# Windowed attention and a squared-ReLU MLP on one core: how K, Q and V reach TensorE (casting six-row loads for two batches, fp32 loads with engine casts and bf16 transposes for the other six)

## The chip, the cores and the metric

The kernel runs on one core of a Trainium2 chip. The metric is device time in microseconds (us) of one execution; lower is better. The core has five engines that run their own instruction streams in order: TensorE (PE, with its weight loads shown as PEld), VectorE (DVE), ScalarE (ACT), GpSimd (POOL) and SyncE (SP), which here issues DMAs. POOL issues DMAs too, and only POOL's queue converts types on the way.

## The reference, cut to what matters

```python
# q, k, v: (8, 8, 576, 64) float32; global_idx: 8 sorted positions
scores = scale * np.matmul(q, k.transpose(0, 1, 3, 2))
mask = np.abs(pos[:, None] - pos[None, :]) <= 32
mask = mask | is_global[:, None] | is_global[None, :]
scores = np.where(mask, scores, -1000000000.0)
attn = softmax(scores)                              # over the keys
attn_out = np.matmul(attn, v)
x = attn_out.transpose(0, 2, 1, 3).reshape(4608, 512)
h = x @ w_in                                        # (512, 2048)
r = np.maximum(h, 0.0)
out = (s * (r * r) + b) @ w_out                     # (2048, 512), float32
```

Each query sees the keys within 32 positions and the 8 global keys; the 8 global queries see every key. The attention output of all heads is the input of the MLP.

## The kernel before, in words

**Padding.** The 576 positions of a batch are cut in five chunks (`NCH`) of 120 keys (`KC`). A chunk takes 128 rows: rows 0 to 7 hold the 8 global keys, rows 8 to 127 the chunk's own. For queries the 8 global rows sit in the middle, at rows 60 to 67. So a band of scores, chunk by chunk, holds the window and the globals together, and a multiplicative mask of zeros and ones (`masks`, one for each chunk) takes care of the rest.

**Pairs.** The work of attention is cut in 32 pairs `p`, two heads of one batch each (`bi, hp = divmod(p, 4)`). `run_pair` has eight steps `s`: steps 0 to 4 are the five chunks (`qk`: one matmul into `pss`, an exponential on ACT into `e`, the mask product on DVE into `em`); step 5 transposes K of the next pair (`trans_a`), step 6 transposes Q of the next pair (`trans_b`), step 7 multiplies by V (`pv`, into `po`). Normalisation (`norm_steps`: `ln`, `rep` on ACT, `xt` on DVE) of a pair is spread over steps 1, 3 and 4 of the next one. In batch 0, `select_globals` fetches the 8 global K and Q rows by one-hot matmuls in fp32 (`psg`), and `select_v` does it for V (`psv`).

**Row loads.** `natk` and `natq` are fp32 tiles, double buffered, filled by SP DMAs of 64-element runs (`load_k`, `load_q`); V goes by casting POOL DMAs straight into `vbufs`, a bf16 tile that holds beside each head's 64 columns 64 ones, so that `pv` gives the row sums as well. K and Q are transposed in fp32 by TensorE with an fp32 identity; ACT and DVE copy the transposes to bf16 (`kt`, `qbd`). For batches 1 to 7 the global rows come from small DRAM buffers (`gsk`, `gsq`, `gsv`), written by 24 gathers on POOL with positions held in registers, and are put into place by `fill`.

**MLP.** `moe_quanta` yields 288 quanta of four 512-column matmuls, for nine tiles of 512 tokens: per tile 16 quanta of the first product (`psh`, ReLU on ACT into `r`, square on DVE into `g`), then 16 of the second (`pso`, four of them for each 128 output rows, which DVE scales into `osb` and SP stores). `Q(n)` emits n quanta between the steps of attention, as far as the budget `quanta` allows. A tile can start when the batches that it covers have been finished by `finish_batch`, which divides the sums of the global queries and lets POOL write 8 columns of `xt`.

**Order.** The order on each engine is the order in the program, written out by hand (`manual_schedule`). DVE work of a step is collected in `later` and emitted one step later. The program is: transposes for pair 0; pairs 0 to 3 without quanta; `finish_batch(0)`; 14 quanta, with `weights_out` between them (w_out arrives in fp32 through two staging buffers, ACT casts it to `wout_t`, DVE adds it up in `wsum` for the bias row); pairs 4 to 7 with three quanta each; pairs 8 to 31 with eight quanta each; 7 quanta; `finish_batch(7)`; the last 64 quanta. Loads of the next batch are emitted ahead of its second pair (`hp == 1`).

PSUM tiles rotate: `ps_s` has two buffers, for scores and transposes; `ps_m` three, for the MLP and the selections; `po` has one.

Of the kernel before, what the change touches and what calls it, by code (L numbers as in the profile page):

```python
# [9 lines left out]
FP32 = mybir.dt.float32  # L10
# [25 lines left out]
PADROW = 96  # L36

# [22 lines left out]
def kernel(  # L60
# [24 lines left out]
    gpa = ctx.enter_context(tc.tile_pool(name="gpa", bufs=1))  # L85
    mop = ctx.enter_context(tc.tile_pool(name="mop", bufs=3))
    wtmp = ctx.enter_context(tc.tile_pool(name="wtmp", bufs=2))
# [24 lines left out]
    natk = [const.tile([P, NCH, H, D], FP32, name=f"natk{i}", tag=f"natk{i}") for i in range(2)]  # L112
    natq = [const.tile([P, NCH, H, D], FP32, name=f"natq{i}", tag=f"natq{i}") for i in range(2)]
    vbufs = [
        const.tile([P, NCH, H, 2 * D], BF16, name=f"vx{i}", tag=f"vx{i}") for i in range(2)
    ]
    qbufs = [const.tile([P, 2, LQ], BF16, name=f"qbd{i}", tag=f"qbd{i}") for i in range(3)]
    HG = H // 2
    for half in range(2):
        hs = slice(HG * half, HG * half + HG)  # L120
        nc.vector.memset(natk[0][:, :, hs], 0.0)
        nc.gpsimd.memset(natq[0][:, :, hs], 0.0)
        if half == 0:
            nc.gpsimd.memset(vbufs[0][:], 1.0)  # L124

    rowi = const.tile([P, 1], FP32)
    nc.gpsimd.iota(
        rowi[:], pattern=[[0, 1]], base=0, channel_multiplier=1,
        allow_small_or_imprecise_dtypes=True,
    )  # L130
    kidx = const.tile([P, NCH], FP32)
    nc.gpsimd.iota(
        kidx[:], pattern=[[KC, NCH]], base=0, channel_multiplier=0,
        allow_small_or_imprecise_dtypes=True,
    )
    WM = P + 2 * WIN
    iot = const.tile([P, WM], FP32)
    nc.gpsimd.iota(
        iot[:], pattern=[[1, WM]], base=-WIN, channel_multiplier=0,
        allow_small_or_imprecise_dtypes=True,  # L140
    )
    identf = const.tile([P, P], FP32)
    make_identity(nc, identf[:])


    def load_k(eng, bi, h0, nh):
        d = natk[bi % 2]
        for c in range(NCH):
            n = min(KC, S - KC * c)
            eng.dma_start(  # L150
                out=d[NG : NG + n, c, h0 : h0 + nh],
                in_=k[bi, h0 : h0 + nh, KC * c : KC * c + n].rearrange("h s d -> s h d"),
            )

    def load_q(eng, bi, h0, nh, part):
        d = natq[bi % 2]
        for c in range(NCH):
            a = KC * c + HB * part
            n = min(HB, S - a)
            r = (HB + NG) * part  # L160
            eng.dma_start(
                out=d[r : r + n, c, h0 : h0 + nh],
                in_=q[bi, h0 : h0 + nh, a : a + n].rearrange("h s d -> s h d"),
            )

    def load_v(bi):
        d = vbufs[bi % 2]
        for c in range(NCH):
            n = min(KC, S - KC * c)
            nc.gpsimd.dma_start(  # L170
                out=d[NG : NG + n, c, :, 0:D],
                in_=v[bi, :, KC * c : KC * c + n].rearrange("h s d -> s h d"),
            )

    load_k(nc.sync, 0, 0, HG)
    load_q(nc.scalar, 0, 0, HG, 0)
    load_q(nc.sync, 0, 0, HG, 1)
    load_v(0)
    load_k(nc.sync, 0, HG, HG)
    load_q(nc.sync, 0, HG, HG, 0)  # L180
    load_q(nc.sync, 0, HG, HG, 1)

# [5 lines left out]
    b_bc = const.tile([P, 1], FP32)  # L188
    nc.sync.dma_start(out=s_bc[:], in_=_bcast_dram(moe_s[:], P))
    nc.sync.dma_start(out=b_bc[:], in_=_bcast_dram(moe_b[:], P))  # L190

    w_in2 = moe_w_in.rearrange("(a p) f -> p a f", p=P)
    for j in range(4):
        nc.gpsimd.dma_start(
            out=win_t[:, :, 512 * j : 512 * j + 512],
            in_=w_in2[:, :, 512 * j : 512 * j + 512],
        )
    w_out2 = moe_w_out.rearrange("(a p) n -> p a n", p=P)
    wst = []
    for j in range(2):  # L200
        wt = wtmp.tile([P, 4, DM], FP32, tag="w", name="wo")
        nc.sync.dma_start(out=wt[:], in_=w_out2[:, 4 * j : 4 * j + 4])
        wst.append(wt)

    greg_p = [
        nc.gpsimd.value_load(g32[:1, i, 0:1], min_val=0, max_val=S - 1) for i in range(NG)  # L206
    ]


    gidx_f = const.tile([P, NG], FP32)  # L210
    nc.vector.tensor_copy(out=gidx_f[:], in_=g32[:, :, 0])
    grow = const.tile([P, 1], FP32)
    nc.vector.tensor_scalar(
        out=grow[:], in0=rowi[:], scalar1=float(NG) - 0.5, scalar2=None, op0=OP.is_le
    )
    koff = const.tile([P, 1], FP32)
    nc.vector.tensor_scalar(
        out=koff[:], in0=grow[:], scalar1=-100000.0, scalar2=-float(NG), op0=OP.mult, op1=OP.add
    )
    nc.vector.tensor_tensor(out=koff[:], in0=koff[:], in1=rowi[:], op=OP.add)  # L220

    qhi = const.tile([P, 2], FP32)
    nc.vector.tensor_scalar(
        out=qhi[:, 0:1], in0=rowi[:], scalar1=float(HB) - 0.5, scalar2=-100000.0,
        op0=OP.is_ge, op1=OP.mult,
    )
    nc.vector.tensor_scalar(
        out=qhi[:, 1:2], in0=rowi[:], scalar1=float(HB + NG) - 0.5, scalar2=100000.0 - NG,
        op0=OP.is_ge, op1=OP.mult,
    )  # L230
    nc.vector.scalar_tensor_tensor(
        out=qhi[:, 0:1], in0=qhi[:, 0:1], scalar=rowi[:], in1=qhi[:, 1:2],
        op0=OP.add, op1=OP.add,
    )
    qidx = const.tile([P, NCH], FP32)
    nc.vector.tensor_scalar(
        out=qidx[:], in0=kidx[:], scalar1=qhi[:, 0:1], scalar2=None, op0=OP.add
    )
    nc.vector.tensor_scalar(
        out=kidx[:], in0=kidx[:], scalar1=koff[:], scalar2=None, op0=OP.add  # L240
    )
    selk = const.tile([P, NCH, NG], FP32)
    selq = const.tile([P, NCH, NG], FP32)
    for sel, idx in ((selk, kidx), (selq, qidx)):
        nc.vector.tensor_tensor(
            out=sel[:], in0=view(idx[:], [1, NCH], [0, NG]),
            in1=view(gidx_f[:], [0, NCH], [1, NG]), op=OP.is_equal,
        )
    selb = const.tile([P, NCH, NG], BF16)
    nc.vector.tensor_copy(out=selb[:], in_=selk[:])  # L250
# [457 lines left out]
```

## Time and profile before

| what | value |
|---|---|
| time, median of 3 runs (lowest to highest) | 438.45 us (438.01 to 438.61) |
| the profiled execution | 437.67 us; span 436.0 us |
| PE busy | 387.0 us, 89% of the span |
| DVE busy | 265.6 us, 61% |
| ACT busy | 206.7 us, 47% |
| POOL busy | 84.5 us, 19% |
| DMA | 42.00 MB in 128367 packets, mean 96 GB/s |

The page gives busy time by engine, the span in 40 slices, the DMA queues, the chain of work that ended last, and the costliest groups of instructions as "line engine operation, output <- inputs, shapes, count | busy us, mean ns of one | idle time before, and what ended it". The mean of one is a duration; pipelined instructions start closer together than that. Other views used below are the timeline (start, us, engine, line, operation), the chain in order of time (start, us, what) and busy times in windows.

### The profile page before, as it was taken

The numbers are of one execution on the slowest core, as the hardware profiler recorded it, in microseconds if no ns is written. First come the engines' busy times: TensorE is split into PE (matmuls) and PEld (weight loads), VectorE is DVE, ScalarE is ACT, GpSimd is POOL, SyncE is SP. The second block draws the span as 40 slices with busy tenths as digits, with TensorE's granted clock in tenths as the row PEclk, the third lists the DMA queues.
The fourth block names the chain that finished last, engine by engine and source line by source line (L and its number), as shares of the span: only waits on it lengthen the run. The fifth ranks groups of instructions, "written<-read, shape, count | busy, mean of one in ns | idle before, by whom it ended". The sixth has DMA issues, their size and how long they took to land.

```text
span 436.0 us, 8254 instructions
## 1 busy us (share of the span) xinstructions
PE 387.0 (89%) x3063; PEld 241.8 (55%) x3063; DVE 265.6 (61%) x650; ACT 206.7 (47%) x405; POOL 84.5 (19%) x162
## 2 busy tenths in 40 slices
PE   1686984869799999999999999999999999999996
PEld 1563761325455655775577568656755665554442
DVE  7817443597776766676677567666766775442432
ACT  1013321855556733763476447645754673360530
POOL 9744932005005001300310050005000100100000
PEclk9999999989999999999999999999999999999999
DMA  8999194499519911991396169419941000101001
GB/s 134 154 229 257 13 147 58 170 193 97 55 48 151 150 46 67 157 143 52 88 147 111 50 122 148 75 57 138 140 86 50 26 0 30 71 2 65 31 26 72
DMA packets 128367, 42.00 MB, mean 96 GB/s; under 512 B 118655, under 2 KB 120703, under 8 KB 128327
## 3 DMA queue, kind: packets, MB, share of 16 engines
q1 hardware_dynamic: 83724, 34.00, 40.7%
q0 software_dynamic: 43328, 7.16, 24.1%
q8 instruction: 24, 0.39, 0.4%
q10 hardware_dynamic: 1275, 0.31, 0.4%
q14 instruction: 16, 0.13, 0.1%
HBM read 38.82 MB, written 9.83 MB: 112 GB/s over the span
## 4 chain that ended last, share of the span: by engine, by line
issue 49%; PE 30%; POOL 10%; ACT 5%; DVE 4%; POOLq 1%; DMA 1%; ACTq 0%; DVEq 0%
PE psh L518 10%; PE pso L533 10%; POOL vx L170 4%; POOL xt L498 3%; PE psg L391 3%; PE po L450 3%; PE pst L349 2%; ACT e L427 1%; ACT r L525 1%; PE pss L423 1%; DMA wo<-in_moe_w_out_dram 1%; POOL vx L124 1%; ACT kt L363 1%; POOLq L206 1%; DVE vx L417 1%
## 5 line engine op out<-in xcount | busy, mean ns | idle before, releaser
L518 PE MATMUL psh<-xt,win_t 128*128 128x512 bf16 (+7 forms) x1024 | 145.5, 289 | 15.8 <-POOL xt L498 12.3
L533 PE MATMUL pso<-wout_t,g 128*128 128x512 bf16 x576 | 141.1, 379 | 0.0
L525 ACT ACTIVATE r<-psh 128x512 bf16<-128x512 f32 x144 | 89.5, 627 | 80.7 <-PE psh L518 77.8
L427 ACT ACTIVATE e<-pss 128x384 bf16<-128x384 f32 (+1 forms) x160 | 75.5, 484 | 106.6 <-PE pss L423 105.4
L518 PEld LDWEIGHTS <-win_t 128*128 128x128 bf16 x1024 | 86.8, 98 | 62.6 <-issue 21.3
L528 DVE TENSOR_TENSOR g<-r 128x512 bf16<-128x512 bf16 x144 | 60.6, 424 | 53.8 <-ACT r L525 51.8
L533 PEld LDWEIGHTS <-g 128*128 128x128 bf16 x576 | 55.3, 98 | 55.9
L430 DVE TENSOR_TENSOR em<-e,mask 128x384 bf16<-128x384 bf16 (+1 forms) x160 | 54.6, 342 | 36.8 <-ACT e L427 35.5
L498 POOL COPY xt<-xg 128x4 bf16 x72 | 15.7, 218 | 271.9 <-DVE xg L496 239.1
L423 PE MATMUL pss<-qbd,kt 128*128 128x384 bf16 (+1 forms) x160 | 51.4, 337 | 12.1 <-POOL qbd L302 4.0
L542 DVE SCALAR_TENSOR_TENSOR osb<-pso,s_bc,bias_row 128x512 f32<-128x512 f32 x36 | 26.9, 747 | 31.8 <-PE pso L533 31.8
L381 DVE CAST qbd<-pst 64x512 bf16<-64x512 f32 x64 | 44.1, 689 | 2.1 <-PE pst L349 1.2
L450 PE MATMUL po<-em,vx 128*64 128x160 bf16 (+3 forms) x896 | 37.1, 233 | 3.1 <-DVE vx L417 1.7
L450 PEld LDWEIGHTS <-vx 128*64 128x64 bf16 x896 | 29.7, 117 | 14.5 <-issue 7.9
L349 PE MATMUL pst<-identf,natk 128*128 128x128 f32 x160 | 30.0, 295 | 8.7 <-DMA natk<-in_k_dram 8.6
L170 POOL DMA_DIRECT2D vx<-in_v_dram x40 | 35.3, 897 | 3.2 <-issue 3.2
L349 PE MATMUL pst<-identf,natq 128*128 128x128 f32 x160 | 28.8, 298 | 5.7 <-ACT kt L363 4.8
L349 PEld LDWEIGHTS pst<-identf,natk 128*128 128x128 f32 x160 | 20.9, 150 | 18.7 <-POOL identf masks.py:199 8.6
L481 DVE TENSOR_TENSOR xt<-po,rep 128x600 bf16<-128x600 f32 x32 | 25.1, 783 | 8.6 <-ACT rep L479 8.6
L423 PEld LDWEIGHTS <-kt 128*128 128x128 bf16 x160 | 15.5, 100 | 25.8 <-DVE qbd L381 6.1
L363 ACT CAST kt<-pst 128x512 bf16<-128x512 f32 x32 | 20.1, 629 | 18.2 <-PE pst L349 18.2
L349 PEld LDWEIGHTS pst<-identf,natq 128*128 128x128 f32 x160 | 19.7, 150 | 11.6 <-ACT kt L363 9.1
(75 smaller groups left out, 202.0 us busy)
## 6 DMA issues: line engine op xcount, KB each, us to landing
out_dram<-osb SPq DMA_DIRECT2D x36, 256.0 KB
natq<-in_q_dram SPq DMA_DIRECT2D x63, 120.0 KB
natk<-in_k_dram SPq DMA_DIRECT2D x28, 240.0 KB
wo<-in_moe_w_out_dram SPq DMA_DIRECT2D x4, 1024.0 KB
vx<-in_v_dram POOLq DMA_DIRECT2D x32, 120.0 KB, 8.4
win_t<-in_moe_w_in_dram POOLq DMA_DIRECT2D x4, 512.0 KB, 15.5
natk<-in_k_dram SPq DMA_DIRECT2D x7, 192.0 KB
natk<-in_k_dram SPq DMA_DIRECT2D x8, 120.0 KB
```

Of the source, the lines that this page charges most:

```text
L170: nc.gpsimd.dma_start(out=d[NG : NG + n, c, :, 0:D], in_=v[bi, :, KC * c : KC * c + n].rearrange("h s d -> s h d"),)
L349: nc.tensor.transpose(ps[:, dst0 : dst0 + P], src2(src)[:, c, P * hp : P * hp + P], identf[:])
L381: nc.vector.tensor_copy(out=qdst(p, hh, 0, 512), in_=ps[r])
L423: nc.tensor.matmul(ps[:], ktile[p][:, P * c : P * c + P], qbufs[p % 3][:, :, LO[c] : HI[c]])
L427: nc.scalar.activation(e[:], ps[:], AF.Exp, scale=SCALE)
L430: later.append(lambda: nc.vector.tensor_mul(em[:], e[:], masks[c][:]))
L450: nc.tensor.matmul(po[D * hh : D * hh + D, a : a + n], vx[:, c, 2 * hp + hh, D * part : D * part + D], emt[(p, c)][:, hh, x : x + n], star ...
L498: nc.gpsimd.tensor_copy(out=xt[:, :, ds(greg_p[i], 1)], in_=xg[:, :, i : i + 1])
L518: nc.tensor.matmul(psh[:, d0 : d0 + n], win_t[:, a, f * P : f * P + P], xts[bi][:, a, x0 : x0 + n], start=(a == 0 and j == 0), stop=(a == ...
L525: nc.scalar.activation(r[:], psh[:], AF.Relu)
L528: later.append(lambda g=g, r=r: nc.vector.tensor_mul(g[:], r[:], r[:]))
L533: nc.tensor.matmul(pso[:], gl[f][:, u * P : u * P + P], wout_t[:, f], start=(f == 0), stop=(f == 15),)
```

## The change

The computation and the tiling in chunks, pairs and quanta stay. What changes is how data reach the engines, and the order around it.

1. Batches 0 and 1: K and Q come by casting POOL DMAs, six consecutive rows of a head to a partition (96 partitions, 1536 bytes read in one run, `load_six`), into bf16 tiles. 12 transposes of 96 x 64 for a pair, and two short ones for the padding columns, go to a bf16 PSUM tile; the copy out of PSUM puts the columns in order again (`trans`, `evac`). K is copied by DVE; of Q one head is copied by DVE and the other by ACT.
2. The global rows of batches 0 and 1 come by one-hot products in bf16 (24 small matmuls for K and Q of a pair, five for V); the selected V rows go by an SP DMA from `gv` into `vbufs`. The gathers are left for batches 2 to 7, and are issued after `finish_batch(0)`.
3. Batches 2 to 7: K, Q and V come by fp32 SP DMAs into one tile each (`nat`, single buffered), in halves of four heads, 43 DMAs a batch (`fetch`, at the first pair of the batch before; for batch 2 at pair 5). ACT casts K and Q half by half into bf16 (steps 1 and 4 of pairs with `hp` 2 and 3), POOL casts V (step 5). Transposes are bf16 with 128 columns, ten for a pair; DVE makes all copies out of PSUM.
4. V of batches 0 and 1 comes by fp32 SP DMAs, one for each head, and POOL casts it. The ones beside V are gone; the row sums use a constant tile `onesb`.
5. The set-up on DVE is rewritten (masks of half the size, read through a view that repeats them; built after the first copies); the large fills of `natk`, `natq` and `vbufs` go, one of 8 partitions x 2560 elements in fp32 (`nat["v"][0:NG]`) comes on DVE.
6. w_out comes by casting POOL DMAs. The bias sum reads w_out once more, in fp32, in eight pieces on SP (`wpiece`, two staging buffers), two ahead of each of pairs 6 to 9; DVE adds them in the pair after. The 512 rows of tile 0 are held in SBUF until the bias row is there (pair 11).
7. Quanta: 4 instead of 14 before pair 4; 5 instead of 3 in each of pairs 4 to 7; 8 instead of 7 after the last pair.

The diff, cut to its core:

```diff
-    natk = [const.tile([P, NCH, H, D], FP32, ...) for i in range(2)]
-    natq = [const.tile([P, NCH, H, D], FP32, ...) for i in range(2)]
+    nat = {t: const.tile([P, NCH, H, D], FP32, ...) for t in "kqv"}
...
+    def load_six(t, bi, hp):
+        hs = slice(2 * hp, 2 * hp + 2)
+        nc.gpsimd.dma_start(
+            out=six(t, bi)[:, hs].rearrange("p h j d -> p h (j d)"),
+            in_=src[t][bi, hs].rearrange("h (p j) d -> p h (j d)", j=NJ),
+        )
...
+    new_casts(0)
+    load_six("k", 0, 0)
+    load_six("q", 0, 0)
+    for h in range(H):
+        load_v_head(0, h)
...
+    nc.vector.memset(nat["v"][0:NG], 0.0)
...
+    G = nc.gpsimd.tensor_copy
+    cast_v(G, 0, 0, 2)
+    for hp in (2, 3):
+        load_six("k", 0, hp)
+        load_six("q", 0, hp)
+    cast_v(G, 0, 2, 2)
...
+    def trans(t, p):
+        bi, hp = divmod(p, 4)
+        ps = ps_s.tile([P, LQ], BF16, tag="s", name="pst")
+        hc = slice(P * hp, P * hp + P)
+        if bi < 2:
+            for j in range(NJ):
+                for hh in range(2):
+                    nc.tensor.matmul(
+                        ps[D * hh : D * hh + D, NP6 * j : NP6 * j + NP6],
+                        six(t, bi)[:, 2 * hp + hh, j], ident[:NP6, :NP6], is_transpose=True,
+                    )
...
+        else:
+            for c in range(NCH):
+                nc.tensor.transpose(
+                    ps[:, P * c : P * c + P], natural(t, bi)[:, c, hc], ident[:]
+                )
...
-        for i, (src, sel) in enumerate(((natk[0], selk), (natq[0], selq))):
-            for c in range(NCH):
-                nc.tensor.matmul(
-                    ps[:, i], src2(src)[:, c, P * hp : P * hp + P], sel[:, c], ...
+        for i, t in enumerate("kq"):
+            for j in range(NJ):
+                for hh in range(2):
+                    nc.tensor.matmul(
+                        ps[D * hh : D * hh + D, i], six(t, bi)[:, 2 * hp + hh, j],
+                        sel6[:NP6, j], ...
...
+    def select_v(p):
...
+        def put():
+            nc.vector.tensor_copy(out=gv[:], in_=ps[:NG].rearrange("g h d -> g (h d)"))
+            nc.sync.dma_start(
+                out=vx[0:NG, :, 2 * hp : 2 * hp + 2].rearrange("g c h d -> g c (h d)"),
+                in_=view(gv[:], [0, NCH], [1, 2 * D]),
+            )
...
+    def casts_for(bi):
+        return (
+            {1: [lambda: cast(A, "k", bi, 0, HG)], 4: [lambda: cast(A, "q", bi, 0, HG)],
+             5: [lambda: cast_v(G, bi, 0, HG)]},
+            {1: [lambda: cast(A, "k", bi, HG, HG)], 4: [lambda: cast(A, "q", bi, HG, HG)],
+             5: [lambda: cast_v(G, bi, HG, HG)]},
+        )
+
+    def fetch(bi):
+        for h0 in (0, HG):
+            load_kv(nc.sync, "k", bi, h0, HG)
+            load_q(nc.sync, bi, h0, HG)
+            load_kv(nc.sync, "v", bi, h0, HG)
+            if h0 == 0:
+                for t in "kqv":
+                    fill(t, bi)
...
     quanta[0] = 32
-    for j in range(4):
-        Q(3)
-        weights_out(j)
+    for _ in range(3):
+        Q()
         flush()
-    Q(2)
-    flush()
     trans_a(4)
     trans_b(4)
+    select_globals(4)
+    select_v(4)
+    Q()
     flush()
...
     for p in range(4, 4 * B):
         bi, hp = divmod(p, 4)
-        nq = [1] * 8 if bi > 1 else [0, 1, 0, 1, 0, 1, 0, 0]
...
-        if hp == 1 and bi + 1 < B:
-            load_v(bi + 1)
-            prefetch_hw(bi + 1)
-        run_pair(p, nq, p + 1 < 4 * B)
+        nq = [1] * 8
+        if bi == 1:
+            nq = [0, 1, 1, 0, 1, 0, 1, 1]
+        elif hp == 0:
+            quanta[0] += 32
+        ex = {}
+        if hp == 0 and bi + 1 < B:
+            if bi > 1:
+                new_casts(bi + 1)
+                fetch(bi + 1)
+        if p == 5:
+            new_casts(2)
+            fetch(2)
+        if hp >= 2 and bi + 1 < B:
+            ex = casts_for(bi + 1)[hp - 2]
+        if p in (7, 8, 9, 10):
+            more, adds = adds, []
+            for s, f in zip((2, 3, 6, 7), more):
+                ex.setdefault(s, []).append(f)
+        if p in (6, 7, 8, 9):
+            for j in (2 * p - 12, 2 * p - 11):
+                adds.extend(wpiece(j))
+        if p == 11:
+            ex.setdefault(0, []).append(bias)
+        run_pair(p, nq, p + 1 < 4 * B, ex)
```

More of the change, by code (lines that the diff above doesn't have):

```diff
@@ new lines @@
+    for hp in (2, 3):
+        load_six("k", 0, hp)
+        load_six("q", 0, hp)
+    cast_v(G, 0, 2, 2)
+    for j in range(4):
+        nc.gpsimd.dma_start(
+            out=win_t[:, :, 512 * j : 512 * j + 512],
+            in_=w_in2[:, :, 512 * j : 512 * j + 512],
+        )
+    cast_v(G, 0, 4, 2)
+    cast_v(G, 0, 6, 2)
+    greg_p = [
+        nc.gpsimd.value_load(g32[:1, i, 0:1], min_val=0, max_val=S - 1) for i in range(NG)
+    ]
+    new_casts(1)
+    for hp in (0, 1):
+        load_six("k", 1, hp)
+        load_six("q", 1, hp)
```

475 lines of the change are left out of this document (222 added, 253 removed).

## The prediction

> **What bounds the kernel now.** I read the page's slices first, then busy times by window, then the chain in order of time. Page:
>
> ```profile
> PE   1686984869799999999999999999999999999996
> ```
>
> Windows (busy us and count by engine, granted clock, DMA share, GB/s):
>
> ```profile
> 150.00:200.00 50.00, 48.45 (x440) 30.66 (x437) 33.69 (x86) 28.23 (x58) 6.00 (x13) 1.00 0.75 99
> 82.00:85.00 3.00, 2.49 (x13) 1.03 (x12) 0.54 (x2) 2.81 (x4) 0.00 (x0) 1.00 0.96 332
> 193.00:196.00 3.00, 2.83 (x37) 1.84 (x36) 2.42 (x8) 1.32 (x3) 0.00 (x0) 1.00 0.74 105
> 196.00:199.00 3.00, 3.00 (x27) 1.48 (x23) 1.19 (x3) 0.91 (x3) 0.00 (x0) 1.00 0.05 10
> ```
>
> From slice 10 on PE is full (48.45 of 50) while ACT has 28 and DVE 34: there the time is PE's own instructions. The first 96 us are not PE-bound. The chain:
>
> ```profile
> 20.18 0.44 PE pss L423
> 31.80 3.07 DVE vx L417 x5
> 37.62 0.46 PE pss L423
> 40.39 1.09 PE pst L349 x4
> 43.25 4.07 PE psg L391 x20
> 47.32 1.74 PE po L450 x16
> 49.06 0.39 PE pss L423
> 60.43 0.39 PE pss L423
> 72.67 5.00 PE psh L518 x12
> 80.11 5.03 DMA wo<-in_moe_w_out_dram
> 94.75 1.71 PE psb L654 x2
> 96.45 0.59 PE pss L423 x2
> 173.57 0.21 POOL xt L498
> 215.03 0.20 POOL xt L498
> 376.80 13.97 PE psh L518 x128
> 432.26 0.75 DVE osb L542
> ```
>
> Pair 0 begins at 20.2, pair 1 at 37.6 (V's selection and its copies lie between), pair 2 at 49.1, pair 3 at 60.4, the MLP at 72.7, pair 4 at 96. Of a pair's 11.4 us, 4.07 are fp32 selections. 14 quanta take 24 us, with a wait for w_out. From there a batch takes 215.03 - 173.57 = 41.46. The tail from 376.80 to the span's end, 59.2, stays as it is.
>
> The timeline, in a steady pair for PE and ACT, in the first stage for DVE and ACT:
>
> ```profile
> 174.73 1.04 PE L450 MATMUL po<-em,vx 128*64 128x160 bf16 x28
> 175.70 1.05 PE L518 MATMUL psh<-xt,win_t 128*128 128x128 bf16 x8
> 176.58 0.30 PE L423 MATMUL pss<-qbd,kt 128*128 128x320 bf16 x1
> 177.59 0.33 PE L423 MATMUL pss<-qbd,kt 128*128 128x384 bf16 x1
> 181.71 0.60 PE L349 MATMUL pst<-identf,natk 128*128 128x128 f32 x4
> 182.15 1.04 PE L518 MATMUL psh<-xt,win_t 128*128 128x128 bf16 x8
> 183.57 0.66 PE L349 MATMUL pst<-identf,natq 128*128 128x128 f32 x4 [0.17 <-ACT kt L363]
> 132.34 1.00 PE L518 MATMUL psh<-xt,win_t 128*128 128x448 bf16 x7 [1.07 <-POOL xt L498]
> 181.56 0.66 ACT L525 ACTIVATE r<-psh 128x512 bf16<-128x512 f32 x1
> 182.03 0.51 ACT L427 ACTIVATE e<-pss 128x320 bf16<-128x320 f32 x1
> 38.58 0.74 DVE L430 TENSOR_TENSOR em<-e,mask 128x320 bf16<-128x320 bf16 x2 [1.01 <-ACT e L427]
> 40.77 0.47 ACT L427 ACTIVATE e<-pss 128x320 bf16<-128x320 f32 x1
> ```
>
> From start to start: PV 0.97, a quantum 0.87, a score chunk 0.15, an fp32 transpose 0.11 (0.44 for four), plus 0.17 waiting for ACT's copy. Per pair 0.97 + 8 x 0.87 + 0.75 + 1.1 + 0.2 = 10.0, four of them 39.9; 1.07 for the global columns makes 41.0 of the 41.46.
> In the first 70 us the same instructions are slower: four transposes 1.09 on the chain, and the first 12 MLP matmuls 5.00 (0.42 each) against 13.97 for 128 (0.11, of half the columns on average) in the tail: half the rate. I price a stage by rows of that stage.
>
> **The change, part by part.**
>
> *Set-up.* Rows that price it (groups):
>
> ```profile
> L121 DVE MEMSET natk<- 128x1280 f32 x2 | 2.2, 1125 | 1.4 <-PEq L692 1.2 <-issue 0.2
> L313 POOL DMA_DIRECT2D gsk<-in_k_dram x8 | 4.6, 574 | 10.5 <-DMA win_t<-in_moe_w_in_dram 9.3 <-issue 0.9
> L479 ACT ACTIVATE rep<-ln 128x640 f32<-128x640 f32 x32 | 24.4, 762 | 0.1
> L381 DVE CAST qbd<-pst 64x512 bf16<-64x512 f32 x64 | 44.1, 689 | 2.1 <-PE pst L349 1.2
> L600 ACT CAST wout_t<-wo 128x2048 bf16<-128x2048 f32 x4 | 7.6, 1905 | 0.3 <-DMA wo<-in_moe_w_out_dram 0.3
> ```
>
> POOL issues two loads (0.6 each by the gathers' row) instead of 7 us of fills, and its index rows are there at about 3.3. DVE then needs some 6.8: 2.3 for the new fill of 2560 elements (twice L121), the rest small instructions of 0.1 to 0.5. Copies of the transposes, about 0.8 each (L381, for 600 elements), and 0.6 of selected columns: pair 0 at 12.2. Five half masks (896 elements) and four fills (640 each) stand on DVE ahead of the first mask product: at L121's 0.88 ns an element 3.0, and 0.1 each to start, 3.9. Five products (0.37 each) and K's copy follow before PV can start, at 18.5; PV's 1.8 covers Q's copies. So pair 1 starts at 20.4, not 37.6.
>
> *Pairs 1 to 3.* Up to the last exponential nothing changes: 40.77 + 0.47 is 3.6 after pair 1's start. K and Q take 14 transposes each, then come 24 selections, five for V, and PV. I price a small one at 0.065, the spacing of PV's 28 (1.74 to 1.8) in this stage: Q's 0.9, selections 1.56, V 0.55, PV 1.8, hence 3.6 + 0.1 + 4.8 = 8.5, against 11.4. No row has a 64-column load with eight columns; the fp32 one's 0.2 (4.07 for 20) is the upper bound, +3.2 a pair; PV's spacing in steady pairs, 0.035 (0.97 for 28), the lower, -1.7. I keep the stage's own row. Pair 3 at 37.4; plus 72.67 - 60.43 = 12.2: the MLP at 49.6.
>
> *To pair 4.* Three quanta 5.0 (the chain's x12), 57 small matmuls 2.9, a quantum 0.9: pair 4 at 58.4 instead of 96.3, with ten quanta (8.7) still owed. w_out's casts leave ACT; its load is the last of some 13 MB on the early queues: at 200 GB/s, an estimate between the windows' 105 and 332, it ends at 65 and is needed at 78, in pair 6; at 150 GB/s it would cost 9.
>
> *Batch 1.* PE: 0.75 + 1.0 + 0.8 + 0.3 + 0.97 + 5 x 0.87 = 8.2, say 8.3: pairs 5 and 6 at 66.7 and 75.0. Here SP's order decides. Its timeline for one batch before:
>
> ```profile
> 173.32 6.08 SPq L150 DMA_DIRECT2D natk<-in_k_dram  x5
> 179.49 12.53 SPq L161 DMA_DIRECT2D natq<-in_q_dram  x10
> ```
>
> A batch of K, Q and V, part by SP and part by POOL, takes from 173.3 to about 195.5 (the windows fall from 105 to 10 GB/s): 22 us, and I take the same 13824 runs at that on one queue. `fetch(2)` reaches SP when pair 5's V rows have gone, at about 65.8. The V rows of pair 6 are queued behind its 43 DMAs: issued at about 87, landed at 89. PV of pair 6 was due at 83. PE stalls 6; ACT's wait for K's first half (with its global rows, at about 79) lies inside. Pair 7 at 91.3, pair 8 at 99.8.
>
> *Pair 9.* `fetch(3)` starts when the last piece of w_out ahead of it has its buffer, at 97.5, and ends at 119.5; the two pieces after it land at about 122.5. But DVE is to add them in step 2 of pair 9, at 111, ahead of masks, squares and copies: DVE stands 11.4, PE about 11 with what it runs ahead and the cold restart. If the DMAs were twice as fast, both stalls would vanish; at half the rate the two cost 22 more each.
>
> *Steady batches.* Ten transposes at bf16: from below 0.056 (a 128-column part of a quantum: 13.97/128 halved), from above the fp32 row's 0.11. I take 0.06, as the part is bf16 with the same columns; the upper end adds 24 x 0.5 = 12. ACT's wait goes (-0.2). The MLP tile now starts a pair after the global columns are written, so the 1.07 goes too. Pair: 0.97 + 6.96 + 0.75 + 0.6 = 9.28. ACT loses K's copy (0.6) and gains two casts of 1280 elements in two of four pairs: 1905 less 768 x 0.83 gives 1.27, about 1.17 start to start. The pair that has eight ReLUs (0.47 to 0.5 from start to start) and both casts needs on ACT 8 x 0.5 + 5 x 0.36 + 1.2 (ln and rep, 0.76 less overlap) + 2.34 = 9.4, as much as PE; followed step by step with two score and three MLP buffers, PE loses 0.6. DVE's copies stay near 2.4 a pair. Loads: K's first half with its globals is there 13 after the fetch began (half of 22, and 2 to land), needed after 21 (two pairs and a step). The stores behind a fetch wait up to 20, covered by three `osb` buffers. POOL's two V casts of about 1.3 may hold DVE once each, inside slack. With the 0.5 that my sum missed before: 37.1 + 0.6 + 0.6 = 38.3 a batch, 37.2 the last.
>
> *Sum.* Pair 8 at 99.8; pair 9 at 109.1; pair 10 at 129.4; pair 11 at 139.3; batch 3 at 150.3 (1.7 for the bias product, moved here); four batches 153.2: 303.5; the last 37.2: 340.7; eight quanta 6.9; tail 59.2: span 406.8. The profiled execution took 437.67 with a span of 436.0, so add 1.7: 408.5. The median stood 0.8 above that execution: 409.
>
> **The rivals.**
>
> 1. *No queue stalls*: SP's loads run faster than before, or DVE's add is covered. Then 17 less: 392. For it: with w_out's long runs a window moved 332 GB/s; against it: these runs are as short as before.
> 2. *The start gains less*: small matmuls and loads keep pairs 1 to 3 near 11.4 and batch 1 likewise 2 longer. 3 x 2.9 + 8 = 17: 426. For it: that stage is slow whatever it runs.
> 3. *Steady pairs keep 10.35*, because ACT's casts or DVE's copies take what PE gives back: 24 x 0.8 = 19: 428. For it: ACT at 9.4 of 9.3.
> 4. *The other side: bf16 transposes stay as in the first stage, 0.27 apiece* (1.09 for four). 10 x 0.21 x 24 = 50 and 28 x 0.21 x 8 = 47: about 505, slower. It decides from 0.125 apiece: 464 transposes x 0.065 = 30. Against it: 0.11 in the steady rows even for fp32. The Trainium skill (TensorE: Matmul & The Clock Gate, Part 4) speaks for it: about 275 ns for a bf16 transpose in a kernel, and no warm clock from transposes; by that the sum would be near 505. The trace's 0.11 spacing speaks against.
> 5. *Each ACT cast waits for its load*: six batches, x late each. Slower from x = 5, that is a fetch 13 later than the 22 us seen. Against it: 8 us of margin.
>
> **How the numbers follow.** My forecast (398 to 420) 0.54; rival 1 0.15; 2 0.12; 3 0.12; 4 0.04; 5 0.03. Time: 409. Range 392 to 428: it takes in rivals 1 to 3 and the transposes' upper bound (421). All but 4 and 5, and a little of 3, are faster: 0.91; 0.2% (about what a measurement of this kernel can tell from no change) on either side: 0.02; slower 0.07.
>
> **What would show it.** Pair 0's first score near 12, pair 1 near 20, the first MLP matmul near 50, pair 4 near 58; PE idle some 6 ahead of PV of pair 6, released by the DMA of the V rows; DVE idle some 11 on a w_out piece in pair 9; batches 38.3 apart; transposes 0.06 apart in steady pairs. The prediction is wrong if SP gets past a fetch in much under 22, if the strided copies take far over 0.8, or if ACT ends the waits in steady pairs.

## The result, and the profile after

| | before | after |
|---|---|---|
| median of 4 runs, us | 438.23 (437.75 to 438.61) | 419.62 (419.16 to 420.05) |
| profiled execution and its span | 437.67, 436.0 | 419.66, 418.0 |
| mean granted PE clock | 0.996 | 0.958 |

The ratio is 0.9576, with a 95% interval of 0.9559 to 0.9592. The direction was forecast; the time is 10.6 above the predicted 409 and inside the range of 392 to 428. Of one kernel below, `all_four`, one of the four runs (407.62) was in a slower state; its median counts that run, its ratio does not.

PE in the page's 40 slices, and the clock that it was granted:

```profile
PE   2596483979925889989998999999999999999994
PEclk9998596999975999999999999999999999999999
```

Slices of 9 begin later than the forecast wanted: at slices 6, 11 and 12, counted from 0, PE stands and waits. Windows tell the same; the columns are us, then busy time and count of PE, PEld, DVE, ACT and POOL, granted clock, DMA share, GB/s. Before:

```profile
60.00:80.00 20.00, 11.55 (x67) 5.09 (x64) 8.61 (x19) 8.06 (x14) 2.84 (x8) 1.00 0.79 69
120.00:140.00 20.00, 18.05 (x169) 11.16 (x169) 13.77 (x36) 10.55 (x22) 6.01 (x13) 1.00 0.75 97
160.00:340.00 180.00, 173.72 (x1557) 116.66 (x1556) 121.96 (x304) 98.95 (x203) 25.61 (x60) 1.00 0.74 101
```

After:

```profile
60.00:80.00 20.00, 12.85 (x170) 7.58 (x172) 9.28 (x26) 7.78 (x17) 8.34 (x21) 0.83 0.61 119
120.00:140.00 20.00, 9.68 (x85) 5.79 (x85) 10.29 (x26) 6.84 (x13) 1.25 (x1) 0.66 0.54 153
160.00:340.00 180.00, 174.11 (x1702) 115.67 (x1714) 121.98 (x293) 119.49 (x226) 18.54 (x48) 1.00 0.50 110
```

From 120 to 140 the new kernel keeps PE busy for 9.7 of 20 us where the old one had 18. From 160 on both are full. PE's timeline after, at the forecast's milestones (start, duration, instruction, in brackets the idle time before it and what ended it):

```profile
12.87 0.75 PE L449 MATMUL pss<-qbd,kt 128*128 128x320 bf16 x2 [1.80 <-DVE gv L439]
22.62 0.77 PE L449 MATMUL pss<-qbd,kt 128*128 128x320 bf16 x2
37.16 0.77 PE L449 MATMUL pss<-qbd,kt 128*128 128x320 bf16 x2
47.98 0.59 PE L546 MATMUL psh<-xt,win_t 128*128 128x512 bf16 x1 [5.03 <-POOL xt L524]
57.20 0.46 PE L449 MATMUL pss<-qbd,kt 128*128 128x320 bf16 x2 [1.65 <-DVE gv L439]
68.82 0.58 PE L546 MATMUL psh<-xt,win_t 128*128 128x512 bf16 x1 [6.17 <-POOL xt L524]
91.74 0.61 PE L476 MATMUL po<-em,vx 128*64 128x160 bf16 x14 [0.92 <-DMA vx<-gv]
101.33 0.30 PE L449 MATMUL pss<-qbd,kt 128*128 128x320 bf16 x1
129.34 0.69 PE L360 MATMUL pst<-ident,cq 128*128 128x128 bf16 x5 [11.72 <-ACT e L453]
135.21 0.31 PE L449 MATMUL pss<-qbd,kt 128*128 128x320 bf16 x1 [0.48 <-DVE qbd L397]
```

Pair 0, pair 1, pair 3, the first MLP matmul and pair 4 stand within 2.3 us of 12.2, 20.4, 37.4, 49.6 and 58.4. Then come a wait of 6.17 in pair 4 that was not forecast, a wait of 0.92 in pair 6 where 6 was, pair 8 at 101.3 (99.8), and a wait of 11.72 in pair 9 behind which pair 10 starts at 135.2 (129.4). What stands behind these waits, on POOL, SP and DVE:

```profile
62.25 4.46 POOL L318 DMA_DIRECT2D gsv<-in_v_dram  x8
66.71 2.06 POOL L524 COPY xt<-xg 128x4 bf16 x8
```

```profile
65.31 2.55 SPq L295 DMA_DIRECT2D natk<-in_k_dram  x5
86.95 2.50 SPq L295 DMA_DIRECT2D natv<-in_v_dram  x5
89.56 0.72 SPq L440 DMA_DIRECT2D vx<-gv  x1
100.11 2.80 SPq L295 DMA_DIRECT2D natk<-in_k_dram  x5
121.54 2.48 SPq L295 DMA_DIRECT2D natv<-in_v_dram  x5
124.12 0.94 SPq L696 DMA_DIRECT2D wst<-in_moe_w_out_dram  x2
```

```profile
127.80 0.69 DVE L700 TENSOR_TENSOR wsum<-wsum,wst 128x512 f32<-128x512 f32 x1 [14.35 <-DMA wst<-in_moe_w_out_dram]
```

`finish_batch(0)` is called once before pair 4 and a second time in it; its eight POOL copies of global columns stand behind 24 gathers and reach POOL at 66.7, and the next MLP matmul reads that tile. SP is in `fetch(2)` from 65.3 to 89.5 and in `fetch(3)` from 100.1 to 124.0; pair 6's V rows go out right behind the first, two pieces of w_out right behind the second.

The table gives the first exponential of a pair, from ACT's timeline, for all kernels that follow (their edits are told below). The kernel before is not at the same place in the MLP at pair 4: its batch 1 runs 3 quanta a pair, the new one's 5.

| kernel | 1 | 4 | 5 | 6 | 7 | 8 | 9 | 10 | 11 | 12 | 16 | 31 |
|---|---|---|---|---|---|---|---|---|---|---|---|---|
| before | 38.1 | 96.8 | 104.1 | 111.2 | 117.8 | 124.4 | 135.8 | 146.1 | 156.0 | 165.9 | 207.3 | 363.1 |
| after | 23.1 | 57.5 | 74.1 | 83.1 | 93.9 | 101.7 | 111.0 | 135.6 | 147.7 | 158.0 | 197.0 | 342.1 |
| e1_once | 23.0 | 57.3 | 67.5 | 76.5 | 97.0 | 105.2 | 114.5 | 140.8 | 152.7 | 163.1 | 201.9 | 347.0 |
| e1_gv67 | 23.0 | 57.4 | 67.6 | 76.9 | 94.0 | 109.8 | 119.1 | 144.4 | 156.5 | 166.8 | 205.7 | 350.9 |
| e1_gvpool | 23.0 | 58.4 | 67.0 | 76.1 | 92.8 | 100.9 | 110.2 | 135.7 | 147.8 | 158.1 | 197.0 | 342.0 |
| e2_gvq | 23.0 | 64.3 | 82.1 | 91.2 | 101.0 | 108.7 | 118.0 | 143.9 | 156.0 | 166.3 | 205.3 | 350.5 |
| e12_both | 23.0 | 65.7 | 73.9 | 83.0 | 95.6 | 112.3 | 121.6 | 146.1 | 158.2 | 168.5 | 207.4 | 352.5 |
| e3_wpool | 23.0 | 57.8 | 74.5 | 83.6 | 95.0 | 102.8 | 112.1 | 123.9 | 136.0 | 146.3 | 185.2 | 330.5 |
| e8_addspool | 23.1 | 57.1 | 73.9 | 82.9 | 93.2 | 101.3 | 110.6 | 120.3 | 130.9 | 155.3 | 194.2 | 339.3 |
| all_four | 23.0 | 58.3 | 66.9 | 76.2 | 86.0 | 97.3 | 106.6 | 118.4 | 130.5 | 140.9 | 179.8 | 325.1 |
| best4 | 23.0 | 57.1 | 65.7 | 74.8 | 84.6 | 94.4 | 103.3 | 116.9 | 128.8 | 139.1 | 178.0 | 323.1 |
| best4_q | 23.0 | 56.9 | 65.5 | 74.6 | 84.4 | 95.3 | 104.9 | 116.8 | 128.7 | 139.0 | 177.2 | 320.4 |
| e5_dbltr | 23.0 | 58.4 | 75.2 | 84.2 | 94.9 | 103.1 | 113.0 | 138.5 | 150.7 | 161.5 | 202.1 | 353.8 |
| e6_dblsel | 23.7 | 60.8 | 77.2 | 86.7 | 97.1 | 104.9 | 114.2 | 138.9 | 150.8 | 161.1 | 200.0 | 345.1 |

### The profile page after: what moved, and what is told of

It reads as the page before. It is cut to its first block, busy times and chain, and to the rows that moved or that the text cites. A ratio compares the mean times of both kernels' runs of the same rounds, so it can differ in the third digit from the quotient of the medians.

```text
span 418.0 us, 8890 instructions
## 1 busy us (share of the span) xinstructions
PE 355.6 (85%) x3323; PEld 215.0 (51%) x3354; DVE 243.7 (58%) x595; ACT 216.1 (52%) x401; POOL 67.2 (16%) x150
## 4 chain that ended last, share of the span: by engine, by line
PE 44%; issue 14%; SPq 13%; DMA 10%; DVE 8%; ACT 6%; POOL 3%; POOLq 0%; ACTq 0%; DVEq 0%
PE pso L561 23%; PE psh L546 14%; SPq L295 7%; SPq L306 6%; DMA natk<-in_k_dram 4%; PE po L476 3%; ACT r L553 3%; PE pss L449 3%; DMA win_t<-in_moe_w_in_dram 3%; DMA natv<-in_v_dram 2%; DVE g L556 2%; DVE qbd L397 2%; PE pst L360 2%; ACT e L453 1%; DVE wsum L700 1%
## 5 line engine op out<-in xcount | busy, mean ns | idle before, releaser
L556 DVE TENSOR_TENSOR g<-r 128x512 bf16<-128x512 bf16 x144 | 64.9, 455 | 53.8 <-ACT r L553 51.8
L258 POOL CAST vx<-natv 128x1280 bf16<-128x1280 f32 (+1 forms) x20 | 21.3, 1077 | 98.5 <-DMA natv<-in_v_dram 45.7
L397 DVE COPY qbd<-pst 64x640 bf16<-64x640 bf16 (+1 forms) x56 | 29.4, 525 | 0.3
L495 ACT ACTIVATE ln<-po 128x640 f32<-128x640 f32 x32 | 22.5, 705 | 5.4 <-PE po L476 5.4
L505 ACT ACTIVATE rep<-ln 128x640 f32<-128x640 f32 x32 | 24.4, 764 | 0.1
L476 PEld LDWEIGHTS <-vx 128*64 128x64 bf16 x448 | 17.0, 118 | 14.3 <-issue 5.1
L476 PE MATMUL po<-em,vx 128*64 128x160 bf16 (+3 forms) x448 | 21.7, 237 | 2.5 <-DVE xt L507 1.6
L476 PE MATMUL po<-em,onesb 128*64 128x160 bf16 (+2 forms) x448 | 21.4, 237 | 0.0
L360 PE MATMUL pst<-ident,cq 128*128 128x128 bf16 x120 | 10.8, 222 | 11.7 <-ACT e L453 11.7
L700 DVE TENSOR_TENSOR wsum<-wsum,wst 128x512 f32<-128x512 f32 x14 | 9.6, 685 | 14.4 <-DMA wst<-in_moe_w_out_dram 14.4
```

What stands on the lines that cost most here:

```text
L397: eng(out=o, in_=i)
L476: nc.tensor.matmul(po[D * hh : D * hh + D, a : a + n], onesb[:] if part else vx[:, c, 2 * hp + hh], emt[(p, c)][:, hh, x : x + n], start=k ...
L556: later.append(lambda g=g, r=r: nc.vector.tensor_mul(g[:], r[:], r[:]))
```

## The experiments

All edits are to the changed kernel, times are medians of 4 runs, and each ratio is to the kernel before on the same chip (0.958 means no change against the changed kernel).

**What covers what in batch 1.** Theory: SP's order sets the stage, and the stall on POOL only stands in place of the one that was forecast. Rival: POOL's stall is a price of its own.

```diff
-                if hp == 0 and bi > 0:
+                if hp == 0 and bi > 1:          # e1_once
                     later.append(lambda: finish_batch(bi - 1))
```

> The four POOL copies of batch 0's global columns, written a second time in pair 4, are left out (they write the same values). In the changed kernel PE stood 6.17 us on them in pair 4, because they are queued behind 24 gathers on POOL. My theory (SP's order sets this stage): pair 5 starts near 67.2 instead of 73.3, but the selected V rows of pair 6 are still issued at 89.6, behind fetch(2), so PV of pair 6 waits about 7 instead of 0.9; pair 7 starts at the same 93.6 within 1; time 418.6 to 420. Rival (POOL's queue alone is the price): pair 7 starts near 87.5, time 413.5.

Measured: 420.82, ratio 0.9617 (0.9568 to 0.9665). Pairs 5 and 6 start 6.6 earlier, and pair 6 then takes 20.5. On SP and on PE of this kernel:

```profile
91.07 0.72 SPq L440 DMA_DIRECT2D vx<-gv  x1
```

```profile
83.05 0.42 PE L449 MATMUL pss<-qbd,kt 128*128 128x320 bf16 x1 [4.68 <-ACT e L453]
93.08 1.01 PE L476 MATMUL po<-em,vx 128*64 128x160 bf16 x14 [3.20 <-DMA vx<-gv]
```

The theory held in kind: two waits of 7.9 together, one of them ACT's for batch 2's K, which the expectation had left out, take the place of 6.17. Pair 7 is even 3.1 later, more than the 1 allowed: PV of pair 6 begins 1.3 later (93.08 for 91.74), as its V rows go out 1.5 later, and the rest is PE's slow restart (V's 14 matmuls take 1.01, and 0.61 in the changed kernel; the granted clock from 83 to 99 is 0.50). The biggest wait of PE in batch 1 is thus worth nothing by itself.

Next, the V rows on ACT's queue, alone and with the first edit.

```diff
         def put():
...
-            nc.sync.dma_start(
+            nc.scalar.dma_start(                # e2_gvq, e12_both (with e1_once)
                 out=vx[0:NG, :, 2 * hp : 2 * hp + 2]...
```

> The selected V rows go out on ACT's queue instead of SP's, so pair 6's are not behind fetch(2). My theory: pair 4 still stands 6.2 on POOL's copies, and pair 6's wait of 0.9 to 1.4 goes; time 418 to 419. Rival (SP's order is the real price and POOL's stall only its cover): 413 to 414.

> Both edits: no second writing of batch 0's global columns (same values), and the selected V rows on ACT's queue. My theory (two stalls that cover one another): pair 7 starts at 87.5 to 89 instead of 93.6, time 414 to 416; ACT's cast of batch 2's K, due about 6 us earlier, may take 1 to 2 of it. Rival (the stalls are independent): the sum of the two edits alone. Rival (the start is bounded elsewhere, by loads): no gain, 419.6.

Measured: 426.57, ratio 0.975 (0.9702 to 0.9797), and 428.09, ratio 0.9777 (0.9724 to 0.983): both lose 7.0 and 8.5 where a gain was expected. DVE's and ACT's timelines of the first, at the end of pair 1:

```profile
28.74 0.28 DVE L439 CAST gv<-psv 8x128 bf16<-8x128 f32 x1
```

```profile
34.69 0.70 ACTq L440 DMA_DIRECT2D vx<-gv  x1
35.44 0.82 ACT L453 ACTIVATE e<-pss 128x320 bf16<-128x320 f32 x2 [6.46 <-DMA natv<-in_v_dram]
```

ACT runs in order, so the exponentials of pair 2 stand 6.46 behind the DMA of the V rows. The source of that DMA is not what is late: DVE had written `gv` at 29.0. It waits for the landing of a load of V for batch 1 on SP's queue, with no data in common; why is told below. The edit has a second effect: SP, without the V rows, begins `fetch(2)` at 29.1 and not at 65.3. These two runs therefore don't answer the question. The experiments went on with pairs 6 and 7 alone, on the reading that the V rows of the early pairs had not been ready:

```diff
-            nc.sync.dma_start(
+            (nc.scalar if p in (6, 7) else nc.sync).dma_start(   # e1_gv67, with e1_once
+            (nc.gpsimd if p in (6, 7) else nc.sync).dma_start(   # e1_gvpool, with e1_once
```

> Batch 0's global columns are written once (the same values), and the selected V rows of pairs 6 and 7 alone go out on ACT's queue; all others stay on SP. With all of them on ACT the start lost 5.7 before pair 3 (37.6 to 43.0 at its first exponential and on), as ACT stood on V rows that were not ready; that should be gone here. My theory (two stalls that cover one another): pair 6 starts near 76.5, ACT waits to 80.9 for batch 2's K, PE 4.7, and PV of pair 6 no longer waits: pair 7 at 89 to 91 instead of 93.9 (97.0 with the first edit alone), time 415 to 417.5. Rival (bounded by the loads): pair 7 at 93.5 or later, 419.5.

Measured: 426.9, ratio 0.9761 (0.9725 to 0.9798). Pair 6 starts where it was expected (76.9 for 76.5), but pair 7 at 94.0 and not at 89 to 91, and the time is some 10 above the expected one. SP's own waits show a new one:

```profile
SPq L306 <- DMA vx<-gv: 7.0, 1, 7.0
```

A load of Q for batch 2 stood 7.0 until the V rows' DMA had landed, though they share no data; the fetch ended at 98.6 instead of 89.5, and DVE stood on a w_out piece in pair 7 already. The trace holds the reason. Each DMA counts its landing on a semaphore. In these programs the DMAs of SP and ACT take turns on the same eight semaphores, those of POOL on eight others, and nearly every DMA first waits for its own semaphore, that is for the landing of the last DMA that used it (317 of SP's 329 in the changed kernel). Q's load and the V rows have the same one: ACT issues the V rows at 90.20, the semaphore counts the last of their landing at 92.12, SP issues the load at 92.13, having stood there from 85.2. The wait of 6.46 above is of the same kind: the semaphore of ACT's DMA counts the last of the V load at 34.60, and the DMA goes out at 34.69. How the semaphores were given out, the trace does not tell. POOL's queue was tried next, before this was known:

> As the run with batch 0's global columns written once and the V rows of pairs 6 and 7 on another queue, but that queue is POOL's, not ACT's. On ACT's queue a load of batch 2's Q, with no data in common, stood 7.0 on SP until the V rows' DMA of pair 7 had landed, and the fetch ended at 98.6 instead of 90. My theory (the two stalls cover one another, and the wait of 7.0 came from the queue that I chose): here the fetch ends at 90 to 91, ACT waits 3 to 4.5 for batch 2's K, pair 7 at 90 to 91.5 (97.0 with the first edit alone, 93.9 in the changed kernel), time 414.5 to 417.5. Rival (any queue beside SP's makes SP wait): fetch to 96 or later, 423 or more. Rival (loads bound it): 419 to 421.

Measured: 418.81, ratio 0.958 (0.9526 to 0.9634): no change against 0.9576. The fetch ends at 90.7, so the wait of 7.0 came with ACT's queue; pair 7 starts 1.1 earlier than in the changed kernel (3 was expected; ACT waits 3.39 for K, and PE is slow after 5.16 idle). And what is gained is given back in pair 9:

```profile
129.45 0.69 PE L360 MATMUL pst<-ident,cq 128*128 128x128 bf16 x5 [12.57 <-ACT e L453]
```

Pair 10 starts at 135.7, as in the changed kernel (135.6): `fetch(3)` starts at 99.7 instead of 100.1, so the pieces of w_out behind it land at the same time, and that sets pair 10 whatever happens in batch 1. My 414.5 to 417.5 was wrong for that reason.

**Pair 9: the piece, or the engine that waits for it.**

```diff
     def wpiece(j):
         wt = stage.tile([P, 2, DM], FP32, tag="wst", name="wst")
-        nc.sync.dma_start(out=wt[:], ...)
+        nc.gpsimd.dma_start(out=wt[:], ...)     # e3_wpool
...
-            lambda i=i: nc.vector.tensor_add(out=wsum[:], ...)
+            lambda i=i: nc.gpsimd.tensor_add(out=wsum[:], ...)   # e8_addspool, both forms
```

> The eight loads of w_out's fp32 pieces go out on POOL's queue instead of SP's, so that none is behind fetch(3). My theory: DVE's wait of 14.35 in pair 9 and PE's of about 12 behind it go, with the cold matmuls after it; pair 9 to pair 10 takes 9.5 to 10.5 instead of 24.6; time 404 to 407. Rival (the piece is late because the DMA engines are full with the fetch): the wait shrinks by less than half, time 412 to 418. Rival (the next thing is late, the casts of batch 3 behind fetch(3), due 15 us earlier): 410 to 415.

> The fifteen additions of w_out's fp32 pieces run on POOL instead of DVE; the loads stay on SP, so the piece still lands at 127.7. My theory (what costs is that DVE stands in order, not the late piece): pair 9 to pair 10 takes 9.3 to 10 instead of 24.6, pair 10 to pair 11 9.3 to 10 instead of 12.1, and the bias product at the head of pair 11 then waits for the sums, 1 to 6: 402 to 408. Rival (the casts of batch 3 behind fetch(3) take its place): 410 to 416. Rival (POOL's additions hold DVE up as much as its own): 415 or more.

Measured: e3_wpool 409.19, ratio 0.9384 (0.9319 to 0.945); e8_addspool 416.19, ratio 0.9519 (0.9472 to 0.9565). With the loads on another queue pair 9 takes 11.8 instead of 24.6, and 10.4 (8.4 by the ratios) are kept to the end. The 14.35 are SP's order, not the DMA engines' rate: from 110 to 124 they move 206 GB/s there, and 163 in the changed kernel. The Trainium skill (DMA: Bandwidth & Descriptors, Issuing engines are not separate DMA queues) says that issuing from several engines saves only the time to initiate a DMA, usually small; here that time, 24 for the 43 DMAs of a fetch, is what the piece stood behind (SP takes 0.26 to 0.51 for nearly every one; three stand longer, 4.3 together). The run misses the 404 to 407, as pair 9 and pair 10 (12.1) stay long: with the additions off DVE they take 9.7 and 10.6. But that kernel misses its 402 to 408, since there the wait only moved:

```profile
129.50 5.35 POOL L700 TENSOR_TENSOR wsum<-wsum,wst 128x512 f32<-128x512 f32 x4 [18.50 <-DMA wst<-in_moe_w_out_dram]
```

```profile
142.07 2.07 PE L706 MATMUL psb<-wsum,onesf 128*128 128x512 f32 x2 [11.24 <-POOL wsum L700]
```

The bias product at the head of pair 11 waits 11.24 for the same sums (1 to 6 expected). A late transfer costs nothing until the first in-order engine that needs it: DVE stood from 113.5, and with the sums on POOL PE stood for them from 130.8, 17 us further on.

**All stalls together.** The four edits: e1_once, V rows of pairs 6 and 7 and the pieces on other queues, and each fill of global rows behind its own tensor's first half:

```diff
             for t in "kqv":
+                # loads of t's half, then, in the first half:
+                fill(t, bi)                     # all_four, best4, best4_q
```

> Four edits: global columns of batch 0 written once (same values), V rows of pairs 6 and 7 on ACT's queue, w_out's fp32 pieces on POOL's queue, and each fill with the global rows issued right behind its tensor's first half instead of behind all three. My theory: the three stalls of the start go, pair 7 starts at 85.5 to 87.5, pair 8 at 95, pair 12 at 138 to 140 (146.3 with the pieces alone), time 400.5 to 404 against 409.2. Rival (the fetch itself becomes the bound, since its casts are due earlier): 406 to 409.

> The kernel with four edits at 400.9, with the V rows of pairs 6 and 7 on POOL's queue instead of ACT's. Theory: SP's waits of 2.5 for them go, pair 8 starts at 95 to 96 instead of 97.3: 398.5 to 400.5. Rival (POOL's queue, which also carries the pieces and waits 4.5 for their buffers, holds the V rows): 401 to 405.

Measured: all_four (V rows on ACT) 400.88, ratio 0.9147 (0.9109 to 0.9185); best4 (V rows on POOL) 402.12, ratio 0.9205 (0.9153 to 0.9257), the same within the intervals. The V rows on POOL brought pair 8 from 97.3 to 94.4, as expected, but not the time: 402.12 lies in the rival's 401 to 405, though the delay that the rival names does not show. Pair 9 gives back 1.8 of the 2.9 (13.6 for 11.8), and the runs spread from 399.15 to 404.03. Pair 12 starts at 139 to 141 instead of 158.0. The edits gain 10.4 for the pieces alone, nothing for the first and the V rows without them, and 17.5 to 18.7 together; the fills' place was not tried alone.

**The third pair of a batch.** In the changed kernel a batch takes 38.9 to 39.0 (158.0 to 197.0 the first), its pairs, by PE's first scores, 9.3, 9.5, 10.9 and 9.3. PE around a third pair, whose scores begin at 176.4:

```profile
172.09 0.44 PE L360 MATMUL pst<-ident,ck 128*128 128x128 bf16 x5
172.37 1.04 PE L546 MATMUL psh<-xt,win_t 128*128 128x128 bf16 x8
181.29 0.30 PE L449 MATMUL pss<-qbd,kt 128*128 128x320 bf16 x1 [0.58 <-ACT e L453]
187.34 0.31 PE L449 MATMUL pss<-qbd,kt 128*128 128x320 bf16 x1 [0.48 <-DVE qbd L397]
```

One wait is ACT's, one that of Q's copies on DVE. The edit on top of best4:

```diff
-            {1: [lambda: cast(A, "k", ...)], 4: [lambda: cast(A, "q", ...)], ...
+            {1: [lambda: cast(A, "k", ...)], 4: [lambda: cast(G, "q", ...)], ...   # best4_q, both halves
```

> The same kernel with Q's casts of batches 2 to 7 on POOL instead of ACT. Theory (ACT, with eight ReLUs and both casts, sets the third pair of a batch, 10.9 against 9.3): the third pairs fall to 9.3 to 9.6, a batch from 38.9 to 37.4, five batches: 6.5 to 8 faster than the run beside it. Rival (DVE's copies or its shared data path with POOL set it): the batch stays at 38.5 or more, within 2 of the run beside it.

Measured: 399.29, ratio 0.9144 (0.9075 to 0.9213), against 402.12 beside it; the intervals overlap. In the profiles a batch falls from 38.9 to 38.2 (139.0 to 177.2), a third pair from 10.9 to 10.3. Neither end: K's cast alone still holds the fifth score for 0.58, and only the 0.48 goes. POOL and DVE in its third pair:

```profile
159.18 1.50 POOL L262 CAST cq<-natq 128x1280 bf16<-128x1280 f32 x1 [5.98 <-DMA natq<-in_q_dram]
```

```profile
159.53 1.37 DVE L456 TENSOR_TENSOR em<-e,mask 128x384 bf16<-128x384 bf16 x1
163.22 0.34 DVE L456 TENSOR_TENSOR em<-e,mask 128x384 bf16<-128x384 bf16 x1
```

The mask product takes 1.37 beside POOL's cast and 0.34 without it: part of what ACT gives up, DVE pays, though no wait of PE in this pair ends on DVE.

**The price of a transpose and of a selection.**

```diff
-            for c in range(NCH):                # bf16 transposes, batches 2 to 7
+            for c in 2 * list(range(NCH)):      # e5_dbltr
-            for j in range(NJ):                 # selections, batches 0 and 1
+            for j in 2 * list(range(NJ)):       # e6_dblsel
```

> Each 128-column bf16 transpose of batches 2 to 7 is issued twice, to the same place: 240 more in 24 pairs. My theory (PE sets steady pairs, a transpose costs its spacing of 0.056): +13.4, less 1.5 in the third pairs, where ACT ends a wait: 431 to 433. Rival (0.27 apiece as in the first stage, or by the page's 275 ns): +53 to 66, 472 or more. Rival (ACT or DVE sets the steady pair): under +3, 419.6 to 422.5.

> The selections of global rows of K and Q in batches 0 and 1 are issued twice: 24 more small matmuls in each of 8 pairs, the second writing the same values. My theory (spacing as in the trace: 0.48 for 12 cold, 0.35 warm, hence 0.04 and 0.03 apiece): at most 4 x 0.96 + 4 x 0.7 = 6.6, of which pairs 4, 6 and 7 hide theirs in the stalls of batch 1 and pair 0 hides part behind DVE: +2.5 to 4.5, 422 to 424. Rival (the 0.065 apiece of the prediction): 12.5 in all, +6 to 9: 426 to 429. Rival (none on the path, DVE's copies set the start): within 1 of 419.6.

The page in the first expectation is the one of the Trainium skill that the prediction names. Measured: e5_dbltr 431.02, ratio 0.9835 (0.9787 to 0.9883), +11.4 for 240 transposes, within the expected 431 to 433: 0.048 each on average, with 40.6 a batch (161.5 to 202.1). The first scores of a batch's pairs tell more:

```profile
161.19 0.30 PE L449 MATMUL pss<-qbd,kt 128*128 128x320 bf16 x1
171.04 0.30 PE L449 MATMUL pss<-qbd,kt 128*128 128x320 bf16 x1
180.98 0.30 PE L449 MATMUL pss<-qbd,kt 128*128 128x320 bf16 x1
191.88 0.31 PE L449 MATMUL pss<-qbd,kt 128*128 128x320 bf16 x1
```

The first pair takes 9.85 where the changed kernel takes 9.30, that is 0.055 for each of ten transposes, their spacing in the trace. The third takes 10.90 where it took 10.92: ten more cost nothing there. So a bf16 transpose costs its spacing in the pairs that PE sets, and third pairs are set by ACT, and by DVE behind it.

`e6_dblsel`: 422.36, ratio 0.9663 (0.9624 to 0.9703): +2.7. PE's rows in its pair 1:

```profile
27.66 0.80 PE L408 MATMUL psg<-sel,ck 96*64 96x8 bf16 x24
28.32 0.78 PE L408 MATMUL psg<-sel,cq 96*64 96x8 bf16 x24
```

From start to start 24 take 0.66, that is 0.028 apiece and not 0.065. Pair 0's are hidden: its first score stands at 12.87 in both kernels. Pairs 1 to 4 lose 0.6, 0.6, 0.9 and 1.2, together 3.3, the last two more than 0.66 as PE is slower there (a granted clock of 0.50 from 36 to 40). Pair 12 starts 3.1 later, so the selections of pairs 5 to 7 are covered by the waits there.

## Why the prediction was right or wrong

The terms, as the traces put them (measured less predicted, on PE's first score of a pair): pair 8 +1.5; pair 9 to 10 +4.3 (24.6 for 20.3); pair 10 to 11 +2.2; pair 11 to 12 -0.7; four batches +2.5 (155.7 for 153.2); the last batch -1.2; eight quanta +0.7; the tail +1.8 (1.6 of it from the end of DVE's last row to the end of the span, 4.6 for 3.0). Together 11.1; the spans, 418.0 and 406.8, differ by 11.2. Two rows of the changed kernel's start, the masks on DVE and PE's first transposes for pair 1, to which the first point refers:

```profile
12.80 2.58 DVE L246 SCALAR_TENSOR_TENSOR mask<-band,notg,gadd 128x160 bf16<-128x160 f32 x5
18.00 0.69 PE L348 MATMUL pst<-ident,ck 96*64 96x96 bf16 x12 [2.70 <-ACT e L453]
```

- *The start, right in sum.* Pair 1 came 2.2 late. Pair 0 was 0.7 late already. The masks took 2.6 where the forecast's prices give 1.3, but the four fills behind them 1.6 where they give 2.7, so that the two add only 0.3. The rest was not in the sum: PE's own transposes and selections for pair 1, 2.9 from 18.00 on, were taken to run ahead, and stood behind ACT's exponentials, which waited for DVE's mask products and so for the set-up. From pair 1 to 2 and from 2 to 3 it took 7.6 and 7.0 instead of 8.5: small matmuls were priced at 0.065, and the selections stand 0.028 apart in e6_dblsel. The two errors cancel. The 57 small matmuls ahead of pair 4 were put at 2.9, which is 0.05 apiece and not 0.065; they took 1.8.
- *Batch 1, right place by luck.* The step that failed is the order of the queues: every queue that a step depends on has to be followed, and I followed SP's and not POOL's, where the copies of the second call of `finish_batch(0)` stand behind the gathers. PE's stall of 6.17 came two pairs before the one I named. The sum for pair 8 held within 1.5 because that stall covered the forecast one. e1_once, where it is gone, has the forecast wait, split between ACT and PV, and there pair 8 starts at 104.8 by PE's first score, 5.0 above the forecast's 99.8. The sum itself holds 8.0 for the stall (91.3 less 75.0 and 8.3), not the 6 that it names.
- *Pair 9, right mechanism, two terms under-sized.* DVE stood 14.35 where 11.4 was forecast (a fetch took SP 24 and not 22, and began 2.6 later), and pair 9 lost 15.3 with PE's slow restart where 11 was in the sum. The granted clock from 129 to 133 is 0.50. e3_wpool and e8_addspool show the cause: either edit takes DVE's wait out of pair 9.
- *Pair 10* was taken as steady with 0.6 more. It took 12.1. e8_addspool, 10.9 by PE's first scores, puts 1.2 of that down to the additions on DVE, which the sum had not priced at all; the 10.9 left are those of a third pair, below.
- *Steady pairs, nearly right.* The transposes stand 0.055 apart in the trace (five take 0.44, one 0.22, hence 0.22 / 4) and cost 0.055 in the pairs that PE sets (e5_dbltr); 0.06 was forecast. Third pairs lose 1.6 and not 0.6: the second wait, DVE's copies of Q behind ACT's casts, was missed, and ACT's first cast alone costs 1.0 (10.3 in best4_q, where Q's is gone). That is 4 x 1.0; the rest of the batches came 1.5 under.
- *The rivals.* Rival 1 (no stalls, 392) did not come; with the stalls removed by hand the time is 399 to 402. Rivals 2 and 3 did not come. Rival 4, transposes at 0.27 apiece, fell: the Trainium skill (TensorE: Matmul & The Clock Gate, Part 4) gives about 275 ns and no warm clock, and the trace has a duration of 219 ns but a spacing of 55, at a granted clock of 1.00 among other matmuls. A duration is not a price where instructions overlap. Rival 5 stayed small: batch 2's cast of K found its load, but only because pair 4 had stalled; with that stall gone ACT waited 3.39 for it (e1_gvpool).

## What to carry to other kernels

Price a moved DMA by its place in the issuing engine's order: list for each queue what is issued ahead, and find the first in-order engine that needs the data. Stalls in a row that hang on one queue cover one another; taking away the largest wait of a profile can gain nothing until the last one of the chain goes, so remove them together before judging any. Moving an issue to another engine's queue puts that engine's own work behind whatever the DMA waits for: its source, and any earlier DMA that shares its semaphore.

## What the runs showed of the hardware that was not expected

- POOL and DVE hold one another up: in best4_q a mask product of 0.34 took 1.37 and ended 0.2 after POOL's cast, and a square of 0.42 took 2.83 beside two casts in a row. In the changed kernel V's casts do it already (squares of up to 1.46); such a cast takes 1.25 alone and up to 1.51 where a DVE instruction had begun first. The products into `xt`, with one input in PSUM, keep their 0.78 beside a cast. The Trainium skill (SBUF — State Buffer, Who interferes with whom) says that a VectorE instruction with two SBUF inputs contends with a GpSimd instruction that reads SBUF, and that the loser waits for the whole instruction; the 1.37 beside the cast's 1.50 agrees.
- After an idle PE of 5 to 12 us the same matmuls run slower for a while: five transposes 0.69 instead of 0.44, V's 14 matmuls 1.01 instead of 0.61, and the window from 120 to 140 has a granted clock of 0.66. A stall costs more than its length here: 15.3 for a wait of 11.72 on PE. The record of the clock does not tell all of it: from 20 to 30 it stands at 1.00, and there 12 transposes of batch 0 take 0.69, which take 0.45 from 33 on.
- A DMA issued on ACT's queue made SP wait 7.0 for its landing, with no data in common, and one on ACT's queue itself waited for SP's load; from POOL's queue neither came. This is the program's doing and not a queue's: SP and ACT share eight semaphores for landings, POOL has others.
